# Attention heads in units of three instead of two: transposes of P, products with V, V rows at a pitch of 40, and a new order

## The chip, the cores and the metric

The kernel runs on one core of one Trainium2 chip. The metric is the device time of one execution in microseconds, the median of the runs shown; lower is better. TensorE (PE) does the matrix products and transposes, VectorE (DVE) and ScalarE (ACT) work between PSUM and SBUF, GpSimd (POOL) and SyncE (SP) issue DMAs.

## The reference

Four layers follow one another on x of 2048 rows by 512: attention A, gated FFN B, A again, B again, each with a layer norm before it and its input added. A walks over 64 segments of 32 rows. Each segment is joined to 8 memory rows, and the memory rows of the next segment are the first 8 output rows of this one, so the segments must be done in turn.

```
for s in range(n_seg):                      # 64, one after another
    h = concatenate([mem, xs])              # 8 + 32 = 40 rows
    q, k, v = h @ Wq, h @ Wk, h @ Wv        # 32 heads of 128
    p = softmax(where(mask, q k^T * scale, -1e9))
    o = (p v) @ Wo
    mem = o[:, :8]; outs.append(o[:, 8:])
B: (sigmoid(x w_gate) * (x w_up)) @ w_down  # 512 -> 1792 -> 512
```

## The kernel before

**Steps.** `emit_step` (L858) does one step: segment t of the first attention layer and segment t - 6 of the second side by side, as 2 x 40 = 80 columns. There are 70 steps; steps 6 to 63 hold both layers, the first and last six one layer. All weights of A lie in SBUF; the FFN weights are streamed by POOL in pieces (L1152, L1153, L1177). `ffn` (L1113) runs for four segments at a time (a block), and its matmuls, the V passes of coming blocks (`v_pass`, L716) and the layer norms are what TensorE can do while a step waits for itself.

**Heads.** The 32 heads are taken as 16 units of two: head u and head u + 16. Three units make a group of six heads, so a step has five groups of six and one of two (L497 to L499). For a group: Q and K (L935), copied to `qku` by ACT; scores (L970); on DVE mask, maximum, subtraction (L984, L989, L991), exponential on ACT (L994), sum, reciprocal, product (L996, L998, L1001), which leaves P in `pb` with each head in 64 columns; one transpose a unit (`ptr`, L1013), which turns the two heads of a unit to partitions 0 to 39 and 64 to 103; two copies (`spread`, L1017) to `ptsb`, which put each head in columns of its own and zero in the rest (`lower` is 0 above the second head's rows, 1 below); the products with V (`pvm`, L1040), one a unit and layer; a copy to `otsb`; and the output projection (L1058). The sum of all heads gives the next step's memory rows (L1071).

**V rows.** `vsb` holds the V rows that a step multiplies: three tiles of half the heads, two used a step. The second head of a unit lies 64 partitions below the first. Rows of x are computed ahead by `v_pass` and lie in DRAM (`scr`); eight DMAs a step with both layers fetch them (L904). The memory rows and the rows around them are computed in the step (`strips`, L849: 32 matmuls into four strips of 32 partitions, eight heads each), copied to the one tile `sst`, and sent to `vsb` by eight DMAs (L915) in the order of halves.

**Order.** Every task (some instructions on one engine) has dependencies, and the list SEQUENCE, a packed permutation, gives each a priority. `forward` (L287) plays the tasks through with planned durations, always taking the first in priority that can go, and so sets each engine's program order. Where the plan leaves TensorE waiting over 250 ns and its use around that gap is under 60%, `warm` (L432) puts matmuls on the tile `hot` in (at most 512 columns each, shown at L1283), which compute nothing that is used.

Of the kernel before, what the change touches and what calls it, by code (L numbers as in the profile page):

```python
# [54 lines left out]
;AsOkoLv9`|Nk$f)V(EM&}eu|$fC*urB1ZmLCVnbIiO{+HzA9)1<7?iu49pb(F}QJGi)Mg^0?ej9TT%>AnXGip&#Uz1Yr8{%{!1PcqJ{qbHL*46O=`m^O8{4Ag{5mcV_X)uOki698u=JbnecdQ)K?*jal`5k@vgq  # L55
O#U-a+Y~cLsg}0BaD;=R(uf~+cDuOTj@JKC;Rp|!BSTrXhnGGEu2%?g?J3{5u2N_9c4_%y>Rv3GR3tbZ)35VLYb%41oUy#Ihn<M~Q_0PVJfBAjNN{?ArwdoxQl<8vGoCwW00SsIKwToFeLh}80qVHqyuc{BDH}Ey
{H^GH#mhlWktNfVUA_ObdEE8yLY~EY#;q0uJyla@^F8xlDxTf&iV#}}k%IRd<x89?fY<{VoG&ZiZDAtha3$KRH{_E2=pj7Ub)bKc&g{kv{=p<B33H2I%(GM876q}G|L&{(rXf+CSLenR2oySHQ8ncu>TnKY{XhT1
?TMKCCm-VE^y=fng`^uZ+^sDt13Z<=jDIP{P3xVKz`!ct$wx2qkoT>eyRST`@>$Zc6F@P+mW6XGY9+$Vs<`x|H(D!?ZBEBql0MU9kT4Rr?<%pVq&RX$KUAD(slP|owV&{0j(-#4d*u#-q|9w-%@MpethdTH$qkCd
6|IG;_iy1dNi<{8R<Y-t*Z7AcN`{y1Zc5;TSUhrMfVfA-_-6}JgtI8A#Q1E=b`WOK5^~&mS{dK4ku8CFRO{TIv63+=(P?6CsuH-+?-Q$b*;V;v7g8oR+f?V};zlQm*%~HtiTbPS>i#JSHN&MilwlzAf#lGrX4(5o
JrCuU{~<^*{mnSblJbT~tZg;n6sKkmCneGTjg20ED^mjHd?@}zwiJ}QxH0g5BDw7pD3%0?;2T;EAWpDb?2J~GfZlUEDCCSg0q)`5yKb(GbdD3}^G^OmVj^dF*y@ih1|qzn>2at0(c7q;$}c9252(bzy0&q@E~Sv*  # L60
GXhk);r*_V=wc=7DFhq1t0^|jR*Hm_QlTqOW;fO`YPVL>=v^%wub=xW?P*i1%~Ob!M&(+_FK_e#vFRTC@r8>s#^u<%CZA8iji*hKiCGt?DjdVOn5tH+`KgLfYpiiCwt1w4j-LstcC$+~w;F-=IuU3;1Oq$VvaOVU
_S{vk%=q!AFI?;DuNc4b2yMJ+2*o9xG9ib$oOpD}s7@VYnma-~c{H>^>!GDpwojb;Bk~AstXZ*m`<`^1oc^Ao#v3ALTiO^PvrXJ~Kp#rUkMj6$`bMLe+xGUlSxQ5sO@$l$(B8<vz!~B1)5ZoV<1$<wj*GX?HIYjL
(A3~WrpA$or6&VL_xici_S7a9+v9%=y0hu!p|er(?}aXw{LdjCua%iOF7B4yTzSrHxwdgZF@u4l9m--GD-3T43nLR~TP^CAb_Mvm2n(K6%eA)Hi3mzK_H6`=r|y-#@HXj<!hgX>L~_bBe_^v~n3&Fa;|!BdB$aF^
?UwyG$lcfh@iLd>l@=8<Iye-jrf`vgT+E}lE|IV0(UY)o2daV&{Cheo!bTrqkMEpwnaG8qtrDP&p-sDO#XTJB{6-p(`Z|%6$9d(56?0>}Hnvb;I}1Hcww2uD*w-iv-~3Pv7>ptX+AT|E4mR1+5eZ5$?wttv&uHLR
1dgfX{P5n((GDeT;c$jo&C4ioc`nV}E)U44AaI#?c4xlgWj~q!d3EUFbp@HFP)P!KwmR8Gt7o|+q6N>%0!h{`s!F`1TRo4rdNGu}b4XbS7Y4kZDtGd`F=kM=-X`xYk3{;qj@mdET|`MuNhb^0(FlWjLoFZwlbspr
f*z`Tk!FkgDa0HM5$G%}cr!#+S>=;wt0mLGroaKT_r$I#s7Mhnpa!lC^q$lbH48m3a<sCo#-=q0n*^Sys%L_3+F8-1tPHF_Gx5C&Gf%pg{eXNi)6N01;g=+vhb*;Nnd1b<OfPd`;D#nyxvqiVG|O8#1DS7$<tB^E
NIL3erxaCpiBh4~i`21Sjv+m=yO=O<8GGg)rmuk?+PE)r`4Pz%AHd10rIzDlfC6n)S-|9VpoPePn-Tz7%@bxy(Vo<zW*m&1B<WP{nSREA2Jfs*&7zo&qz{z(4;<s0U|q7yxHgKws=ZLIGY@^C6S%dpL+o!xSP}>~
1^anNE}jYpLB_6(S_Ao8OZgz<WCPa*mZf;~An4=j0~fx(hIAyg`-kss;*I0f>kE)-bmx`Dr%0OpTPKDhv<HGdB^nJWIthe8MJ=!0+3iERRaWt|_pBw*R3T`&%|47GbLRPr8;AGi`9fU0hi9L3RPV>=+YUXM-#e@C
@1A#@s;uT+%_?u?1y}+|vp>>i1^gK<r;enb80tVX9Q!HtL6t;PGOO!&rgWh4wWLr~n(#~=N=4?k&om$D*}zCzdjUPbsE*)!Yli^o=6##Vh(!E*Fv@-R#Lz>+A^AlRl9zz!*<Hc}?ayVBH&JAwms75uI<?T+UkaqQ
UF02QasyU|1;o6=UyH-imTIrGtM=|{sv<}Od)cxP%0K^tLm5;XY@OGucPB%W485G2=`jxAA*A?5jR`^9R`)`ZC0g4Gm$hD=n)&o#<IS7(#|CYXnNOWjBjWdVT01~zIN-epto-Mr=t|R1HemE8#@M<@8?HBtPmw6M  # L70
H~p3D0=P8Kr7lS(@A!8*+J9Vcj_@RpmyYg0Ao=nE&*`{$_xquaS^S7CxtA`#+onhks4U%V_C>Ni>p0VJg1G#<sK70daQ~+!3d0KXjhR@lGe*X(PltJH75(%U+_~RxhVpGQi^4$V{k2taQ{(mXR}(AgnVMKb=m>Z)
ewpv8M}ar=+ak{0UJ!_yRQfmtbx?t3`H~&;{ur58BJp_Cdp1JGBDw5s4e#66qO-^CsbMCep+WUN5}jky#v6OibJ*!g+k#Q~2gnL^Pat**eTqqT#>K{0gCQk%B}dBT2Cg?Q$-L8t8ur4{Xx*jwy%zuqu#j*U&ORwB
q%tQEi-vR?4g6hdG5a1gv>Kuvrht>h@v<tF4ncn+p4&hdUu~=%n=1&Dak36wjj%?XP>O@U&($c)ZRxy9p4h9_t(^Mkw>`<Dg<}|P{KU#!GD3=&^zditEjxaJQ-)d4(uHu@#g&Uz@%xy79+QPaqqTSWQ*>Z8qVL{I
1_#0b2AS)7SZLJpO(uEk)(b+8=BT_q6hR9>RKC4t<m4ME*C=B-Ah?cwDCV8_u?@kLm9L^0P3Gb>X~8^!<n~~H<)qX}UKBd;C4E6t!9d_IcQK1<XqLzV56-mb>Ut5KqX}?hbiw+1aQUP}3+n+|fR!>AHTckh5CHK7
A|^7r4BupK)p1t{D(XlquV)sysuLpa*v68G-#(<b#-S}o*zN-S;OnyrU-7obFX!O|W4%;Uj+GT+T@f9osMr-bv$DwR<e;R@+(rg=u;%sSP-~4CI}ugoIRIQJ16$4{bWtp7ZxU`$zTcqO^0bdrXA@x_NbbnYAVoic
$6#csoA@80l?l`+G0UJb2eQkn+HJc-z{__<nNGs!rMGHd*b;KH=d6~BEkOB@hk6fo3dk8h_H-!@IHEIC1h&o6vx$Ie<qyw<t~&^^pTdz9jW-1r4cqKB<PAq0jPF|VD@w7Wn+$&TX%9~+b0qmb2fO1e6>a<8Q5`R2
>ABezR@U}(@aoA2pz{3u)>l&0ySVhwMRaTg@6J^o?W`>zWTDc~MvENf`u+40C%DKP%Y~L%LyLc|<ikb^YBcUc7j{|@aFg6A=QhL=<F8q{jbWi;bfc~v@SFXQvAo~EnPp9_&VNNdWvs9=PRWhgJ%OkfbiIWe7a7=i
FDmuxoNdd#e4+I99cv2m?Pv2$b2xV+ec^;+HDx}nJun_B?HTr$Rp9Z$Ck~EIJGI;H!~g-koU=YNZ#J^teR1Ix-kqhNMSeJ|!uw?vBqp4RK(I{O{WmSauU+?HaFXM>_=`9&!x2fRJZlxAFN7o=3-WIExWihbgiWIh
7I>W<07<NMXHvJ&Y26oHmqhJNA0`xtbB-1z!S$}U)$O1@B=@ERfx}yW^b}QJ`J8B>{0S2x&05vHXUeg)OJ4{Z?}87ke=_GSohFoUiu%%yoit#ESi@9~_Zd|a(az_UG<MWAgf_q_L0_`<<sM6=jZ(7025qc&cq$D&
dc%HbKfgTkfwDQkbO2m|#)Rn_NYmxV+*q6rqa^_HuF}1hrNP7^N%fFR%7%+p7{i;A#1-pz1Auv)Ufx28PEP8A8w^tnHjYeJBp~3d5Z3`?xxz9kcBua|G}m()#^TbGZNU>@3tClz=-8!ohmh(YSmZUa+c2HlGf2{M  # L80
%=$ceF_)Zv*HLi~=R#=+rN~V3Ejuew4<YmxBOkK->7o$9-rQFVPIn?OZ@YW3ZV=dI9l{Kx$zd^}NA~+QSf6~kdnx(q0gbi&Vz<n}b?1Y}1Y9G{7Pr-JSNv_M$Stl0JvOON;uPce=n;i6-aqMMZ>FNZgZ1SshdoD5
T&a3gEi9*n>qkTsxXsR{`Cr6jz04c$|6IK{r_}#FmMI9Dv0z5ezQdu;`dR+8k4(FxPrI|t3vD}hK-uG}`lrHeh`&4h#R$ikG%sLCw;TG4k5H-Igi*#|$)Pl|Zw+UfyY+MUKw=Hwp!<~oJVk%MzbfAp9YtFqoNWXZ
Vk-{`mfT&9=`-c-7~^<W!jMPR8uXHrsy<C6A~5hpsKj`|Uao&M1>Lw%YnQaeiQs8ti@t2n6<C27iOXVKmL5!;MH;7&wZ}??vXK(qSjE}wIVyRBXbvBZ-IR^T3lK;wBkxq(1`_q<vX3pYpi}0_>0^4S2sxU<X=(n?
)AIBS#-6>k*cd_SHLM~A)v%?kE|XUGLSIk9vPMsu;w?kHH@%}{7Y%>8HfHEgw1fmn3)DCxCT23S$KJ`yST(8CI3Hz@fZ|@KLgW8=fHa32O_&W2IwFZj#`K!W#;8>Ce_$qc8@kVjiFO3I#xit?gotIf2k?R0%%-Ob
lhln?Xi2EdGbl(~!0}0^<CvBVwC*~zt+Uf`=d&>nglS7(n39NVEJe>UPrcl3ktD8OKph~rssP^Xiew@d0z&3ir08G|N=W&03@OViOgG_t=0pKPnZ?9<rG8s|<>Wp&YZCtY;2x9SA1I;hDm^H*!XQj&cBm1c5<|Iv
)Pm74sdZ-+;|L$~max>Sa_w@h=MjVRrAmw?S%dzo>sPWdVfiguEOmvWs&M<xHZ?yf(D!BZydSVEL%}aIaocLLM{o8*U@ub?5td;*!!|M9hY-I}2dXzf!Q7U8iBSa64a|!1&X0nn<3E{uTJ~U=R9njs@urQ@8fS{f
zirfGnyQ4a8suz1z_;)M%kQG5nFV+g{YHeLj5Lq=>;7Y0RS)L|_=NA955WW48wHiH>S{V3Zm}+%4@h@K2g!aahDSWo<BM6w^{YX12ICdYrij-`LW$+|b&|&eCG3Eim{!LRoL%~`$L&Oh`@loZ$`o$pqrg+)T5|(>
$-$PuYQOYl1hM2jZFpiL5T9cJ=)R%`Gd9w-<Apss-226onD;>_t{mc!NbZH(krC+lNKSDeEfDwi9{+fsy(PdkTy;nZ3EF}gbXV9y0h5GW^6gIAswDgt)c10#g`L$exUKvJbfTjQW)}YVQoD>>H(AqhZkO*6v9CI|
_(E@w*FmagFtyfnx$r<RFu_Mg1Byt2598@E+uU9d?$Kon*Jj5lyikh|uFRKl&`w3@r|U%F0|3yo!G~ynrNoEO*MF?OEPQK-=-B|CpyBIe-1cqxK;26#)fH_gTo<j?Q4qPlNoGvqOKv3YU(4=PHxfsIWr4`ZmZM5R
kc+hD>7{*O@<mO;9d&|ZuMT6hIy^B#U}bJ%!btuf`$QrAJ>;<I7Gr~3NRs6{51bo<I)>B+|8+~Mgm}5mF(#yzQM9`pPlVO)=r@Gelq8qoMM-Fir|L@tZ3|e1$9kNp_-|VN+V@Dn0!|(gryFf1P8~SeE6MY$K~M)|  # L90
# [385 lines left out]
class Kern:  # L476
# [126 lines left out]
    def load_weights(self):  # L603
# [10 lines left out]
        for h0, n in ((0, 4), (4, 4), (8, 4), (12, 4), (16, 4), (20, 4), (24, 4), (28, 4)):  # L614
            cs = slice(h0 * P, (h0 + n) * P)
            tk = ld(self.wv[:, :, cs], wv_v[:, :, cs], P * self.DC * n * P * 2, [("wv", h) for h in range(h0, h0 + n)], [("wv", h0 - 8)] if h0 > 4 else [])
            if h0 > 4:
                tk.after = pl.writer[("wv", h0 - 8)]
# [744 lines left out]
```

## Time and profile before

| what | value |
|---|---|
| three timed runs | 1776.6, 1775.84, 1775.11 us |
| median | 1775.84 us |
| span of the profiled execution | 1771.0 us, granted clock 1.000 |
| median less span | 4.8 us |
| PE, PEld, DVE, ACT, POOL busy | 99, 85, 66, 66, 33% |
| L1013, transposes of P | 1120 |
| L1040, products with V | 2048 |
| DMA | 273.43 MB, mean 154 GB/s |

The span runs from the first to the last instruction of the execution that was profiled; what of its own time lies outside the span is not shown, and the timed runs stand 4.8 us above it. PE is TensorE's matmuls, PEld its weight loads, which overlap them. The duration of one matmul includes its way through the pipeline and overlaps the next; in the chain that ended last, matmuls stand with the time from one issue to the next.

### The profile page before, as it was taken

The numbers are of one execution on the slowest core, as the hardware profiler recorded it, in microseconds if no ns is written. First come the engines' busy times: TensorE is split into PE (matmuls) and PEld (weight loads), VectorE is DVE, ScalarE is ACT, GpSimd is POOL, SyncE is SP. The second block draws the span as 40 slices with busy tenths as digits, with TensorE's granted clock in tenths as the row PEclk, the third lists the DMA queues.
The fourth block names the chain that finished last, engine by engine and source line by source line (L and its number), as shares of the span: only waits on it lengthen the run. The fifth ranks groups of instructions, "written<-read, shape, count | busy, mean of one in ns | idle before, by whom it ended". The sixth has DMA issues, their size and how long they took to land.

```text
span 1771.0 us, 92273 instructions
## 1 busy us (share of the span) xinstructions
PE 1755.7 (99%) x40066; PEld 1509.6 (85%) x40066; DVE 1174.8 (66%) x4018; ACT 1166.2 (66%) x3024; POOL 577.8 (33%) x836
## 2 busy tenths in 40 slices
PE   9999999999999999999999999999999999999998
PEld 4678888889888888989898898989889888989886
DVE  4477676777566666766776667667766765676665
ACT  6676766666666666666666667666666666666664
POOL 5413032522333242313334241333324232333432
PEclk9999999999999999999999999999999999999999
DMA  9835254634555464445546453555546444554543
GB/s 354 275 88 169 73 165 138 206 109 130 155 158 162 126 193 134 142 123 164 165 143 184 130 172 107 155 155 169 155 131 192 125 139 127 162 153 136 170 135 108
DMA packets 135113, 273.43 MB, mean 154 GB/s; under 512 B 30778, under 2 KB 68546, under 8 KB 134706
## 3 DMA queue, kind: packets, MB, share of 16 engines
q0 software_dynamic: 56656, 183.09, 34.5%
q1 hardware_dynamic: 78050, 84.43, 16.4%
q8 instruction: 314, 5.14, 1.2%
q14 instruction: 93, 0.76, 0.2%
HBM read 221.78 MB, written 27.07 MB: 141 GB/s over the span
## 4 chain that ended last, share of the span: by engine, by line
PE 96%; DVE 1%; ACT 1%; SPq 0%; issue 0%; DMA 0%; POOL 0%; ACTq 0%; DVEq 0%; POOLq 0%
PE bank L935 33%; PE bank L1058 17%; PE bank L1160 11%; PE bank L724 8%; PE bank L849 7%; PE bank L1183 6%; PE bank L970 4%; PE bank L1040 4%; PE bank L1013 2%; PE bank L684 1%; PE bank L1283 1%; PE bank L1128 1%; SPq L915 0%; DMA vsb<-sst 0%; PE bank L762 0%
## 5 line engine op out<-in xcount | busy, mean ns | idle before, releaser
L935 PE MATMUL bank<-hT,wq_sb 128*128 128x80 bf16 (+3 forms) x8960 | 615.2, 198 | 0.8 <-issue 0.4
L935 PE MATMUL bank<-hT,wk_sb 128*128 128x80 bf16 (+3 forms) x8960 | 614.8, 198 | 0.0
L1297 ACT CAST qku<-bank 128x480 bf16<-128x480 f32 (+3 forms) x770 | 387.3, 506 | 219.3 <-PE bank L935 180.2
L935 PEld LDWEIGHTS <-wq_sb 128*128 128x128 bf16 x8960 | 452.3, 99 | 21.4 <-issue 10.6
L935 PEld LDWEIGHTS <-wk_sb 128*128 128x128 bf16 x8960 | 446.7, 99 | 0.0
L984 DVE TENSOR_TENSOR st<-bank,cst 40x240 f32<-40x240 f32 (+3 forms) x768 | 279.1, 368 | 166.6 <-PE bank L970 160.0
L1058 PE MATMUL bank<-otsb,wo_sb 128*128 128x80 bf16 (+1 forms) x8960 | 361.0, 198 | 1.9 <-ACT otsb L1297 1.1
L1058 PEld LDWEIGHTS <-wo_sb 128*128 128x128 bf16 x8960 | 336.0, 99 | 17.3 <-issue 2.8
L1153 POOL DMA_DIRECT2D wu<-in_B_w_up_dram x217 | 164.0, 756 | 275.8 <-PE bank L1160 91.6
L1152 POOL DMA_DIRECT2D wg<-in_B_w_gate_dram x217 | 164.0, 756 | 234.4 <-PE bank L1160 164.4
L1297 ACT CAST otsb<-bank 128x480 bf16<-128x480 f32 (+3 forms) x420 | 198.0, 483 | 62.1 <-PE bank L1040 43.4
L1177 POOL DMA_DIRECT2D wd<-in_B_w_down_dram x217 | 153.7, 709 | 217.5 <-PE bank L1183 72.0
L994 ACT ACTIVATE st<-st 80x240 f32<-80x240 f32 (+3 forms) x420 | 158.7, 381 | 37.5 <-DVE st L991 34.8
L996 DVE TENSOR_REDUCE small<-st 80x6 f32<-80x240 f32 (+3 forms) x420 | 150.6, 362 | 37.3 <-ACT st L994 35.7
L674 POOL TENSOR_TENSOR small<-small,cst 128x1 f32<-128x1 f32 (+1 forms) x80 | 44.9, 562 | 397.9 <-DVE small L673 392.1
L1160 PE MATMUL bank<-xnT,wg 128*128 128x128 bf16 (+2 forms) x1784 | 171.8, 218 | 0.1
L1160 PE MATMUL bank<-xnT,wu 128*128 128x128 bf16 (+2 forms) x1784 | 171.0, 218 | 0.0
L970 PE MATMUL bank<-qku 128*128 128x80 bf16 (+1 forms) x2240 | 162.2, 198 | 0.4 <-ACT qku L1297 0.4
L991 DVE TENSOR_TENSOR st<-st,small 80x240 f32<-80x240 f32 (+3 forms) x420 | 154.5, 370 | 4.2
L1001 DVE TENSOR_TENSOR pb<-st,small 80x240 bf16<-80x240 f32 (+3 forms) x420 | 153.3, 369 | 4.2
L989 DVE TENSOR_REDUCE small<-st 80x6 f32<-80x240 f32 (+3 forms) x420 | 151.6, 363 | 4.5
L1040 PE MATMUL bank<-ptsb,vsb 104*128 104x80 bf16 x2048 | 136.0, 199 | 2.9 <-DMA vsb<-sst 1.2
(107 smaller groups left out, 2399.6 us busy)
## 6 DMA issues: line engine op xcount, KB each, us to landing
wg<-in_B_w_gate_dram POOLq DMA_DIRECT2D x220, 256.0 KB, 4.3
wu<-in_B_w_up_dram POOLq DMA_DIRECT2D x220, 256.0 KB, 4.1
wd<-in_B_w_down_dram POOLq DMA_DIRECT2D x220, 256.0 KB, 4.1
vsb<-scr SPq DMA_DIRECT2D x460, 48.0 KB
vsb<-sst SPq DMA_DIRECT2D x464, 32.0 KB
scr<-vst SPq DMA_DIRECT2D x112, 96.0 KB
wv_sb<-in_A_Wv_dram SPq DMA_DIRECT2D x8, 512.0 KB
wo_sb<-in_A_Wo_dram SPq DMA_DIRECT2D x10, 384.0 KB
```

Of the source, the lines that this page charges most:

```text
L935: nc.tensor.matmul(o_ap, lhsT=W[:, c, h * P:(h + 1) * P], rhs=mv(c), start=(c == 0), stop=(c == DC - 1))
L970: nc.tensor.matmul(s_all(SB)[:, w0 + i, :], lhsT=fview(qku[:, i, 0, 0:1], [(1, P)]), rhs=qku[:, i, 1, 0:ncol], start=True, stop=True)
L984: pl.add("DVE", dve_ns(n, True), lambda gsz=gsz, hs=hs, st=st, SB=SB, pj_=pj_, npj_=npj_, mk=mk, idx=idx: nc.vector.tensor_tensor(out=st[p ...
L991: pl.add("DVE", dve_ns(n), lambda gsz=gsz, hs=hs, st=st, mx=mx: nc.vector.tensor_tensor(out=st[pr, hs], in0=st[pr, hs], in1=mx[pr, hs].uns ...
L994: pl.add("ACT", act_ns(n), lambda hs=hs, st=st: nc.scalar.activation(out=st[pr, hs], in_=st[pr, hs], func=ACTF.Exp, scale=self.scale), r=s ...
L1040: nc.tensor.matmul(fview(OB[:, o:o + 1], [(ncol, 2), (1, L)]), lhsT=self.vsb[halves[u // 8]][0:64 + L, j, (u % 8) * P:(u % 8 + 1) * P], rh ...
L1058: nc.tensor.matmul(WB[:, c * ncol:(c + 1) * ncol], lhsT=self.wo[:, h, c * P:(c + 1) * P], rhs=otsb[:, hl, 0:ncol], start=(h == 0 and c == ...
L1152: pl.add("POOL", 760, lambda wg=wg, fs=fs: nc.gpsimd.dma_start(out=wg[:], in_=self.wgv[:, :, fs]), r=[("wo", self.H - 1)], w=[gk] + bt, la ...
L1153: pl.add("POOL", 760, lambda wu=wu, fs=fs: nc.gpsimd.dma_start(out=wu[:], in_=self.wuv[:, :, fs]), r=[("wo", self.H - 1)], w=[uk] + bt, la ...
L1160: nc.tensor.matmul(gu[:, 2 * i + k, 0:n], lhsT=W[:, c, i * P:(i + 1) * P], rhs=xnT[:, c, rw], start=(c == 0), stop=(c == DC - 1))
L1177: pl.add("POOL", 760, lambda wd=wd, ip=ip: nc.gpsimd.dma_start(out=wd[:], in_=self.wdv[:, 2 * ip:2 * ip + 2, :]), w=[dk] + (["boot"] if se ...
L1297: nc.scalar.copy(out=dst, in_=src)
```

## The change

Three rows of heads (0 to 10, 11 to 21, 22 to 31) take the place of two; a unit is one head of each row, so there are ten units of three and one of two. Groups are two units, again five groups of six heads and one of two. A unit's P lies in 3 x 40 of 128 columns; one transpose turns three heads to partitions 0, 40 and 80 on; three copies spread them; one product a unit and layer has up to 120 rows and 120 columns. `vsb` becomes two tiles, each with all heads of a step, three rows of heads at a pitch of 40 partitions; no rows between them need zeros any more. The strips keep eight heads of each row in three strips and the other eight in the fourth, so each row gets two DMAs from `sst`: one of 1024 columns and one of 384 or 256. `runs` gives the pieces in which the columns of `wv`, now in the order of the strips, stand for heads in order; the writes to `scr` and the loads of `wv` are cut by it. SEQUENCE is new. The copies from `kx` wait for the step's `hT` as well.

```diff
-        for u in range(0, self.HH, 3):
-            us = list(range(u, min(u + 3, self.HH)))
-            self.groups.append(([h for k in us for h in (k, self.HH + k)], us))
+        self.NU = (H + 2) // 3
+        self.row_heads = [list(range(i * self.NU, min((i + 1) * self.NU, H))) for i in range(3)]
+        for u in range(0, self.NU, 2):
+            us = list(range(u, min(u + 2, self.NU)))
+            self.groups.append(([r[k] for k in us for r in self.row_heads if k < len(r)], us))
+        self.full = 8 * P
...
-        self.NV = 3
-        self.vsb = [c.tile([P, 2, 1024], BF16, name=f"vsb{i}") for i in range(self.NV)]
-        self.pb = [c.tile([LW, HG, 64], BF16, name=f"pb{i}") for i in range(3)]
-        self.ptsb = [c.tile([P, HG, 2, L], BF16, name=f"ptsb{i}") for i in range(3)]
+        self.NV = 2
+        self.vsb = [c.tile([P, 2, self.NU * P], BF16, name=f"vsb{i}") for i in range(self.NV)]
+        self.pb = [c.tile([LW, 2, P], BF16, name=f"pb{i}") for i in range(3)]
+        self.ptsb = [c.tile([P, 2, 2, 3, L], BF16, name=f"ptsb{i}") for i in range(3)]
...
+    def runs(self, k, w):
+        out = []
+        for i, r in enumerate(self.row_heads):
+            n = len(r) - 8
+            for p0, m, s0 in ((0, 4, 8 * i), (4, 4, 8 * i + 4), (8, n, 24 + 3 * i)):
+                lo, hi = max(s0, 4 * k), min(s0 + m, 4 * (k + w))
+                if lo < hi:
+                    h = r[p0 + lo - s0]
...
-            for hf, vh in enumerate(halves):
-                for i in range(0 if j and not s else 2):
-                    h0 = i * self.HH + 8 * hf
-                    pl.add("SP", 430, ...  # vsb[vh][row:row + nx, j, :] <- scr[j], heads h0 to h0 + 7
+            for i, rh in enumerate(self.row_heads):
+                m = len(rh) * P
+                pl.add("SP", 430, ...  # vsb[vh][row:row + nx, j, 0:m] <- scr[j], heads of row i
...
-            for i4 in (0, 2, 1, 3):
-                vh, i = halves[i4 % 2], i4 // 2
+            for k in (0, 1):
                 for j, lo, k0, nr, name in parts:
+                    for i in range(3):
+                        p0, o, m, c = (32 * i, 0, self.full, 0) if not k else (96, 3 * P * i, (len(self.row_heads[i]) - 8) * P, self.full)
+                        pl.add("SP", 632, ...  # vsb[vh][L * i + k0:..., j, c:c + m] <- sb[p0 + lo:..., o:o + m]
...
-                           r=kk, w=[(qku, "e")], use=[qku])
+                           r=kk + hkeys, w=[(qku, "e")], use=[qku])
...
-                    nc.tensor.transpose(out=pt[:, ul * LW:(ul + 1) * LW], in_=pb[full, 2 * ul:2 * ul + 2, :].rearrange("p i k -> p (i k)"),
+                    nc.tensor.transpose(out=pt[:, ul * LW:(ul + 1) * LW], in_=pb[full, ul, :],
...
-            for i in (0, 1):
+            for i in range(ni):
                 def spread(i=i, nu=nu, ptsb=ptsb, PB=PB):
-                    r = slice(0, 64 * i + L)
+                    r = slice(0, L * (i + 1))
...
-                        nc.tensor.matmul(fview(OB[:, o:o + 1], [(ncol, 2), (1, L)]),
-                                         lhsT=self.vsb[halves[u // 8]][0:64 + L, j, (u % 8) * P:(u % 8 + 1) * P],
-                                         rhs=ptsb[0:64 + L, ul * nj + idx, :, :], start=True, stop=True)
-            vk = [(n_, j, vh, i) for vh in sorted({halves[u // 8] for u in us}) for j in jobs for n_ in ("vs", "vx") for i in (0, 1)]
+                        nc.tensor.matmul(fview(OB[:, o:o + 1], [(ncol, ni), (1, L)]),
+                                         lhsT=self.vsb[vh][0:L * ni, j, u * P:(u + 1) * P],
+                                         rhs=ptsb[0:L * ni, ul, idx, 0:ni, :], start=True, stop=True)
+            vk = [(n_, j, vh, i, k) for k in sorted({int(u >= 8) for u in us}) for j in jobs for n_ in ("vs", "vx") for i in range(ni)]
```

More of the change, by code (lines that the diff above doesn't have):

```diff
@@ L595, in clear @@
         for k, t_ in enumerate(self.ptsb):
-            pl.add("POOL", 440, lambda t_=t_: nc.gpsimd.memset(t_[:], 0.0), w=[("ptsb", k, i) for i in (0, 1)])
+            pl.add("POOL", 440, lambda t_=t_: nc.gpsimd.memset(t_[:], 0.0), w=[("ptsb", k, i) for i in range(3)])
         for k, t_ in enumerate(self.qku):
             pl.add("POOL", 440, lambda t_=t_: nc.gpsimd.memset(t_[:], 0.0), w=[("qkz", k)])
-        for k, t_ in enumerate(self.vsb):
-            pl.add("ACT", 1760, lambda t_=t_: (t_[32:64], fview(self.hot[32:64, 0:1], [(0, 2), (0, 1024)])),
-                   w=[(n, j, k, i) for n in ("vs", "vx") for j in (0, 1) for i in (0, 1)])
     def load_weights(self):
@@ L613, in load_weights @@
         xb = list(self.boot_x)[1:]
[L614 to L618, printed above, removed]
+        for k in range(self.H // 4):
+            h0 = 4 * k
+            for o, c0, m, _ in self.runs(k, 1):
+                h1 = h0 + o // P
+                tk = ld(self.wv[:, :, h1 * P:h1 * P + m], wv_v[:, :, c0:c0 + m], P * self.DC * m * 2, [("wv", h) for h in range(h1, h1 + m // P)], [("wv", h0 - 8)] if h0 > 4 else [])
+                if h0 > 4:
+                    tk.after = pl.writer[("wv", h0 - 8)]
             if h0 == 0:
@@ L623, in load_weights @@
             xb = xb[2:]
[L624 to L626 removed]
+        for u0, n in ((0, 2), (2, 4), (6, 5)):
+            hs = [r[u0:u0 + n] for r in self.row_heads]
             for nm, sb, v in (("wq", self.wq, wq_v), ("wk", self.wk, wk_v)):
[L628 to L634 removed]
+                for r in hs:
+                    cs = slice(r[0] * P, (r[-1] + 1) * P)
+                    ld(sb[:, :, cs], v[:, :, cs], P * self.DC * len(r) * P * 2, [(nm, h) for h in r])
+            for r in hs:
+                ld(self.wo[:, r[0]:r[-1] + 1, :], wo_v[:, r[0]:r[-1] + 1, :], P * len(r) * self.D * 2, [("wo", h) for h in r])
+    def runs(self, k, w):
[6 more added lines that the diff above has]
+                    h = r[p0 + lo - s0]
+                    keys = [(i, p0 + q - s0) for q in range(lo, hi)]
+                    if out and out[-1][1] + out[-1][2] == h * P and out[-1][0] + out[-1][2] == (lo - 4 * k) * P:
+                        o, c0, m0, k0 = out.pop()
+                        out.append((o, c0, m0 + (hi - lo) * P, k0 + keys))
+                    else:
+                        out.append(((lo - 4 * k) * P, h * P, (hi - lo) * P, keys))
+        return out
     def first_qk(self):
@@ L891, in s_all @@
             return B[:, 0:6 * ncol].rearrange("p (h k) -> p h k", h=6)
-        halves = [self.nxt("vsb", self.NV) for _ in range(2)]
+        vh = self.nxt("vsb", self.NV)
         alone = not both and t - j0 * LAG in self.thin[j0]
@@ L900, in emit_step @@
             lo, nx = (2 * 8 * j, 8) if alone else (0, XS)
-            for hf, vh in enumerate(halves):
-                for i in range(0 if j and not s else 2):
-                    h0 = i * self.HH + 8 * hf
-                    pl.add("SP", 430, lambda j=j, s=s, row=64 * i + row + lo, h0=h0, vh=vh, r0=s * XS + lo, nx=nx: nc.sync.dma_start(
-                        out=self.vsb[vh][row:row + nx, j, :], in_=self.scr[j][r0:r0 + nx, h0 * P:(h0 + 8) * P]),
-                        r=[("vd", j, b, q, kk) for q in range(lo // 8, (lo + nx) // 8) for kk in (h0 // 4, h0 // 4 + 1)] + ([("wo", self.H - 1)] if t == 0 else []), w=[("vx", j, vh, i)], lat=2700.0, nb=nx * 2048, slow=0.9)
+            for i, rh in enumerate(self.row_heads):
+                if j and not s:
+                    continue
+                m = len(rh) * P
+                pl.add("SP", 430, lambda j=j, row=L * i + row + lo, h0=rh[0], m=m, r0=s * XS + lo, nx=nx: nc.sync.dma_start(
+                    out=self.vsb[vh][row:row + nx, j, 0:m], in_=self.scr[j][r0:r0 + nx, h0 * P:h0 * P + m]),
+                    r=[("vd", j, b, q, (i, k)) for q in range(lo // 8, (lo + nx) // 8) for k in range(len(rh))] + ([("wo", self.H - 1)] if t == 0 else []),
+                    w=[("vx", j, vh, i, k) for k in (0, 1)], lat=2700.0, nb=nx * m * 2, slow=0.9)
         def add_strips(col, parts):
             sb = self.strips(lambda c: hT[:, c, col:col + 32], skeys)
-            for i4 in (0, 2, 1, 3):
-                vh, i = halves[i4 % 2], i4 // 2
+            for k in (0, 1):
                 for j, lo, k0, nr, name in parts:
@@ L1058, in wom @@
                             nc.tensor.matmul(WB[:, c * ncol:(c + 1) * ncol], lhsT=self.wo[:, h, c * P:(c + 1) * P],
[L1059 removed]
+                                             rhs=otsb[:, hl, 0:ncol], start=(h == 0 and c == 0), stop=(h == self.groups[-1][0][-1] and c == DC - 1),
                                              skip_group_check=True)
@@ L1107, in last_weights @@
                     pl.add("POOL", 760, lambda tl=tl, src=src: nc.gpsimd.dma_start(out=tl[:, :, :], in_=src), w=keys, lat=4700.0, nb=370000,
-                           r=[("vs", 1, (2 * (self.NSTEPS - 1) + q) % self.NV, i) for q in range(2) for i in range(2)] if k else [])
+                           r=[("vs", 1, (self.NSTEPS - 1) % self.NV, i, q) for q in range(2) for i in range(3)] if k else [])
                     row.append((tl, own))
```

357 lines of the change are left out of this document (199 added, 158 removed).

## The prediction

> **What bounds the kernel now.** I read the page's busy table first, then the chain that ended last, then the chain inside one ordinary step, then the stages without spare work.
>
> ```profile
> span 1771.0 us, 92273 instructions
> PE 1755.7 (99%) x40066; PEld 1509.6 (85%) x40066; DVE 1174.8 (66%) x4018; ACT 1166.2 (66%) x3024; POOL 577.8 (33%) x836
> PE 96%; DVE 1%; ACT 1%; SPq 0%; issue 0%; DMA 0%; POOL 0%; ACTq 0%; DVEq 0%; POOLq 0%
> ```
>
> TensorE is busy all the time and the chain is TensorE work to 96%; VectorE and ScalarE have a third of the span free. So a matmul less is time less, wherever TensorE is never short of work. The price of a matmul is its step in the chain, not its duration (199 ns for the transposes of P at L1013 and for the products at L1040), because matmuls overlap. The chain between 900 and 926 us, an ordinary step:
>
> ```profile
> 902.52 0.11 PE bank L1013 x3
> ...
> 903.39 0.90 PE bank L1160 x16
> 904.29 0.43 PE bank L1040 x12
> ```
>
> Three transposes take 0.11 us (36.7 ns each), twelve products of 80 columns 0.43 us (35.8 ns each), sixteen FFN matmuls of 128 columns 0.90 us (56.3 ns each). On the line through the last two, 120 columns cost 52.9 ns.
>
> Where there is little other work, the stages differ:
>
> ```profile
> 118.60:135.40 16.80, 16.35 (x498) 13.80 (x494) 10.86 (x41) 12.01 (x46) 2.12 (x3) 1.00 0.29 84
> 175.60:200.10 24.50, 24.50 (x548) 19.41 (x541) 14.98 (x56) 18.35 (x47) 0.17 (x1) 1.00 0.33 91
> 200.10:221.30 21.20, 19.66 (x509) 16.90 (x506) 13.73 (x53) 15.25 (x42) 0.00 (x0) 1.00 0.25 66
> ```
>
> Each line is one step (columns: length, then PE, PEld, DVE, ACT, POOL). Step 6 (second line) has no idle TensorE at all; step 7 (third line), with no FFN beside it, has 1.54 us. In step 3 (first line) part of "busy" is filler: the matmuls on `hot` (L1283) that the code puts where its plan leaves TensorE waiting. The chain of step 7 says what it waits for:
>
> ```profile
> 207.47 1.79 SPq L915
> 209.26 0.05 issue
> 209.31 0.58 SPq L915
> 209.90 0.04 issue
> 209.94 0.59 SPq L915
> 210.53 0.04 issue
> 210.57 3.26 DMA vsb<-sst
> 213.83 0.14 issue
> 213.97 0.56 PE bank L1040 x11
> ```
>
> The V rows of the memory and of the rows around it are computed in the step itself (L849), copied, sent to `vsb` one DMA after another by SP (about 0.6 us each), and land 3.26 us after the last needed issue; only then the first product runs.
>
> **The change part by part.** The order of instructions of the changed kernel gives the counts, the rows above the prices.
>
> Transposes of P: 16 a step become 11, in all 1120 become 770. They still stream 80 columns. 350 x 36.7 ns = -12.8 us.
>
> Products with V: 2048 of 80 columns (73.3 us at 35.8) become 1280 of 120 and 128 of 80 (67.7 + 4.6 = 72.3 us): -1.0 us. The columns are the same; only a fixed part of 768 - 128 = 640 matmuls goes. With V rows at a pitch of 40, 120 rows are contracted instead of 104; the row with 128 rows (56.3 ns) is on the same line, so nothing for that.
>
> A rule is weighed here. The rows give 36 ns at 80 columns, weight load included (85% of PEld is busy beside it). The Trainium skill (TensorE: Matmul & The Clock Gate, "Back-to-back issue gap") says that in a stream of weight loads and matmuls the spacing is set by both, about 81 ns at 128 columns and 131 ns at 512. By a line through these, 74.7 ns at 80 and 79.9 at 120, the two terms would be -26 and -41 us, and the time some 1709 us. The trace disagrees with it at 128 columns, 56.3 against 81 ns, so the sum goes by the rows.
>
> Filler matmuls: 92 become 133, 42,624 columns become 61,184. A filler of 1664 columns takes 0.71 us in the chain at 101.83 us, 0.427 ns a column: 18,560 columns are +7.9 us. They sit in step 6 (+2.5 us), in step 61 (+1.4), in 63, 65, 68 and 69 (+2.8 together), and 0.3 to 0.5 each in the boot, steps 1 to 5 and step 7. These are the places where less TensorE work leaves a wait for something else. Step 6 had no idle time, so its filler is new. Step 7 and steps 65 to 69 had waits already, which filler can only replace. Bounds: 0 (all of it replaces waits) and +10.7 (all new, and each of 14 more filler blocks leaves the 0.2 us that 27 such blocks leave on average now). I take +6.9: step 6 is the nearest row to a fresh wait and its filler counts in full, as do the others but for 1 us that replaces waits the late steps had.
>
> Spread of P (L1017): two copies a group of six heads become three, each of 160 elements instead of 240. From the rows for 80 and 240 elements (ACT 215 and 347 ns plain, 325 and 460 scaled; DVE 187 and 270, 246 and 331) the new ones cost 281, 392, 228 and 289 ns, and with the counts by engine ACT gets +74 us, DVE +12 us over the run, about 1.2 us a step. It is hidden: ACT goes from 66 to 70% of the span, and the last group of a step, which the end of the step hangs on, has two heads and still two copies. Without that cover it would be some 0.25 us a group. 0 on the path; end of the range +4 (0.25 us in sixteen filler-less steps).
>
> V rows: `vsb<-scr` 508 DMAs become 381 (356 ns of SP each), `vsb<-sst` 516 become 774 (587 ns each): SP gets -45 + 151 = +106 us, 1.5 us a step, on a queue that waits over 340 us for L1040 to give `vsb` free. The first product of a step with both layers now waits for six strip DMAs instead of four: 2 x 0.63 = 1.26 us later. What hides it is the TensorE work put between strips and first product. In the order of before, by the rows, that is 6.3 us in step 7, 7.1 in the next, 9.3 in the median; in the changed order 6.7, 7.9 and 11.2. The waits of the last three heads of a unit row (the second piece of 384 or 256 columns) fall on groups 4 and 5, 10.6 us or more after the strips. Two whole-step tiles instead of three halves: a tile is free when the step before the last has done its products, no earlier need than before. I take +0.5 (step 7), end +18 (below).
>
> Boot: up to the first QK of step 1 both orders hold the same V passes, strips and heads; the changed one puts more V passes ahead of step 0, and 1,280 filler columns more (counted above). The three ScalarE clears of `vsb` (1.89 us each) go; they ran beside filler. DMA is full for the first 60 us (share 1.02 to 1.09), and the weights come in other pieces: 0, ends -2 and +3. One more dependence (the kx copies of steps 6 to 11 wait for the step's hT) sits beside the 0.86 us of QK matmuls that the same copy waits for: 0.
>
> Sum: -12.8 - 1.0 + 6.9 + 0.5 = -6.4 us. The profiled execution's span is 1771.0 us; the three timed runs have the median 1775.84, 4.8 us more, which lies outside the span and which I leave alone. 1775.8 - 6.4 = 1769.4 us.
>
> **The rivals.** (a) All of the saving: the added filler only stands where TensorE waited before. For it: steps 7, 61, 65, 68 and 69 had waits. Against it: step 6. -13.8 + 0.5: 1762.5 us.
>
> (b) Nothing gained: with 0.2 us less of TensorE a step, softmax on DVE and ACT becomes what every filler-less stretch waits for, ACT with 1.2 us a step more. For it: step 3, where TensorE needs filler already. Against it: in 903 to 1006 us TensorE is busy 103.00 of 103.00 while ACT is busy 67.13. The sum would be -13.8 + 10.7 + 4 = +0.9: 1776.7 us.
>
> (c) Slower: the V rows come late. Place: the wait of L1040 for `vsb<-sst`. Six issues need 1.4 (strip end to first issue done, as in step 7) + 5 x 0.63 + 2 to 3.3 us of landing = 6.5 to 7.8 us after the strips. It decides when landing under the larger number of DMAs takes 5 us, a need of 9.5: then the ten both-layer steps with 6.7 to 9.0 us between lose 1.26 us each on average, and the eight single-layer steps (5.2 to 6.2 us between, three DMAs first instead of two) 0.63 us each: +18. 1769.4 + 18 = 1787 us. For it: the chain of step 7, and smaller pieces. Against it: the row of L1040 has 1.2 us of idle released by `vsb<-sst` in the whole run, in two places. The Trainium skill (DMA: Bandwidth & Descriptors, "Anatomy of one DMA") says a DMA has about 2 us of fixed cost whatever its size, so that splitting does not make pieces land earlier; the 3.26 us agrees in kind.
>
> That the change does not do what it says is settled by the order: the counts are as told.
>
> **How the numbers follow.** About 0.2% (3.6 us) is what a measurement of this kernel can tell from no change. Forecast 0.48, (a) 0.20, (b) 0.17, (c) 0.15. The forecast's own range, 1764 to 1774, is faster but for its last microsecond or two. Faster 0.66, same 0.17, slower 0.17. The range takes in (a) with the boot's -2 and (b) with its +3, and leaves (c) out: 1760 to 1779.7.
>
> **What would show it.** Right: the transposes at 770 with 37 ns in the chain, products of 120 columns at 53 ns, steady steps 0.2 us shorter with TensorE still full, step 6 longer than that saving by filler. Wrong: idle before L1040 released by `vsb<-sst` in many steps (c); idle TensorE at ACT or DVE in 903 to 1006 us (b); a boot that ends more than 2 us away from 84.3 us.

## The result, and the profile after

The changed kernel is slower: 1797.7 us as the median of its runs beside 1776.2 of the kernel before, a ratio of 1.0128 (95% interval 1.0107 to 1.0149). The forecast was 1769.4 us with a range that ended at 1779.7; rival (c), late V rows, had given 1787. The profiled execution of the changed kernel took 1800.13 us with a span of 1798.3.

The page of the changed kernel, the lines that answer to those shown of before:

```profile
span 1798.3 us, 91097 instructions
PE 1762.6 (98%) x39117; PEld 1504.5 (84%) x39117; DVE 1170.9 (65%) x4093; ACT 1204.4 (67%) x3294; POOL 589.1 (33%) x861
PE 88%; DMA 4%; SPq 3%; DVE 2%; ACT 2%; issue 1%; POOL 0%; DVEq 0%; ACTq 0%; POOLq 0%
```

TensorE has 949 matmuls less and is counted busy 7 us longer. The chain has gone from 96% TensorE to 88%, and what came in is SyncE's queue and DMA, which stood at 0%. The waits of TensorE, longest in total first (us in total, times, longest), say at which line:

```profile
PE bank L1112 <- DMA vsb<-sst: 6.9, 10, 1.2
PE bank L1112 <- issue: 5.3, 4, 2.1
PE bank L1200 <- ACT oxT L1369: 4.3, 11, 0.5
...
PE bank L1112 <- DMA vsb<-scr: 2.6, 2, 1.7
```

L1112 is the products with V. The kernel before had this line for them (L1040):

```profile
PE bank L1040 <- DMA vsb<-sst: 1.2, 2, 0.6
```

So the matmuls were saved, and TensorE now waits for V rows in front of the products; how much of the loss that is, the experiments show. The chain between 921 and 924 us has the prices of the new matmuls:

```profile
923.20 0.07 PE bank L1085 x2
923.27 0.21 PE bank L1112 x4
```

35 ns a transpose, 52.5 ns a product of 120 columns: the forecast had 36.7 and 52.9. If each matmul of the two traces is given its step by columns (columns / 2.4 plus 2.4 ns; strips by their measured step), the sum goes from 1721.6 to 1715.4 us, filler included: -6.2 us. What TensorE took beyond that sum, from its first matmul to its last, went from 44.7 to 78.2 us: +33.5. A gap is here the time from one matmul's issue to the next, less the step of the first; the gaps of over 60 ns in front of products went from 7.3 to 22.7 us in that part.

One step shows the mechanism. The chain in step 14 of the changed kernel (start, us, what):

```profile
393.47 0.07 PE bank L1085 x2
393.54 0.45 PE bank L1232 x8
393.99 0.06 PE bank L1112
394.05 2.08 issue
396.13 0.32 PE bank L1112 x3
```

Between two products TensorE stands for 2.08 us. The page calls it "issue", but the strip transfers of that step tell what it was. On SyncE (durations min, median, max in ns, then first and last start):

```profile
L985 SPq DMA_DIRECT2D vsb<-sst x12: 573/588/1980, 385.9 to 394.8; - x12
```

By the length of their rows they went out as wide, wide, narrow, wide, wide, wide, wide, narrow and four more narrow. Wide is 2048 bytes a row, six of which the first product needs; narrow is 768 or 512 bytes, which only groups 4 and 5 need. The third issue, a narrow one, took 1.98 us. The sixth wide one was issued by 391.7 us, 0.4 us after a 256 KB load of `wu` and just ahead of one of `wg`, and its last part landed 4.35 us after its issue, at 396.0. Then the second product ran.

Step 14 is no exception among the 58 steps with both layers: the six wide transfers stand first in seven of them only, the last of the six is issued 8.3 us after the strips and lands 10.4 us after them (medians; the latest 14.4). In the kernel before, with the order of its instructions laid beside its trace, the last of the four that the first product needs is issued 5.2 us after the strips and lands 7.7 us after them (medians). The prediction had 6.5 to 7.8 us for the landing of the six.

### The profile page after: what moved, and what is told of

Its sections match the earlier page's. It is cut to its first block, busy times and chain, and to the rows that moved or that the text cites. A ratio compares the mean times of both kernels' runs of the same rounds, so it can differ in the third digit from the quotient of the medians.

```text
span 1798.3 us, 91097 instructions
## 1 busy us (share of the span) xinstructions
PE 1762.6 (98%) x39117; PEld 1504.5 (84%) x39117; DVE 1170.9 (65%) x4093; ACT 1204.4 (67%) x3294; POOL 589.1 (33%) x861
## 3 DMA queue, kind: packets, MB, share of 16 engines
q0 software_dynamic: 56992, 182.89, 34.8%
## 4 chain that ended last, share of the span: by engine, by line
PE 88%; DMA 4%; SPq 3%; DVE 2%; ACT 2%; issue 1%; POOL 0%; DVEq 0%; ACTq 0%; POOLq 0%
PE bank L1005 30%; PE bank L1130 17%; PE bank L1232 10%; PE bank L791 8%; PE bank L916 7%; PE bank L1255 5%; PE bank L1112 4%; PE bank L1040 4%; SPq L985 2%; DMA vsb<-sst 2%; PE bank L1085 1%; PE bank L751 1%; PE bank L1355 1%; DMA vsb<-scr 1%; PE bank L1200 1%
## 5 line engine op out<-in xcount | busy, mean ns | idle before, releaser
L1369 ACT CAST qku<-bank 128x480 bf16<-128x480 f32 (+4 forms) x770 | 388.6, 507 | 204.9 <-PE bank L1005 171.4
L1224 POOL DMA_DIRECT2D wg<-in_B_w_gate_dram x217 | 164.0, 756 | 274.5 <-PE bank L1232 169.4
L1225 POOL DMA_DIRECT2D wu<-in_B_w_up_dram x217 | 164.1, 756 | 244.1 <-PE bank L1232 80.0
L1249 POOL DMA_DIRECT2D wd<-in_B_w_down_dram x217 | 154.1, 711 | 181.2 <-PE bank L1255 58.7
L1361 ACT ACTIVATE ptsb<-bank,small 80x160 bf16<-80x160 bf16 (+3 forms) x540 | 186.7, 375 | 22.9 <-PE bank L1085 15.1
L741 POOL TENSOR_TENSOR small<-small,cst 128x1 f32<-128x1 f32 (+1 forms) x80 | 44.7, 559 | 446.3 <-DVE small L740 443.7
L1040 PE MATMUL bank<-qku 128*128 128x80 bf16 (+1 forms) x2240 | 162.8, 198 | 2.8 <-ACT qku L1369 2.7
```

Of the source, the lines that this page charges most:

```text
L1040: nc.tensor.matmul(s_all(SB)[:, w0 + i, :], lhsT=fview(qku[:, i, 0, 0:1], [(1, P)]), rhs=qku[:, i, 1, 0:ncol], start=True, stop=True)
L1224: pl.add("POOL", 760, lambda wg=wg, fs=fs: nc.gpsimd.dma_start(out=wg[:], in_=self.wgv[:, :, fs]), r=[("wo", self.H - 1)], w=[gk] + bt, la ...
L1225: pl.add("POOL", 760, lambda wu=wu, fs=fs: nc.gpsimd.dma_start(out=wu[:], in_=self.wuv[:, :, fs]), r=[("wo", self.H - 1)], w=[uk] + bt, la ...
L1249: pl.add("POOL", 760, lambda wd=wd, ip=ip: nc.gpsimd.dma_start(out=wd[:], in_=self.wdv[:, 2 * ip:2 * ip + 2, :]), w=[dk] + (["boot"] if se ...
L1361: nc.scalar.activation(out=dst, in_=src, func=ACTF.Copy, scale=by)
L1369: nc.scalar.copy(out=dst, in_=src)
```

## The experiments

Ratios are to the kernel before on the same chip; where two experiments are compared, it is by their ratios times 1775.8 us. "Gaps" are those of over 60 ns in front of products, as above, summed from a trace.

**The order of the strip transfers.** TensorE's order is kept, and each slot of SyncE's queue too.

```
+ def wide_first(self, order):
...
+         slots = sorted(at[i] for _, i in ks)
+         new = sorted(ks, key=lambda e: (e[0], at[e[1]]))
...
```

> The changed kernel, with TensorE's order and every slot of SyncE's queue kept, but in the slots that a step's twelve strip transfers hold, the six wide ones (2048 bytes a row, needed by the first product) go first and the six narrow ones (768 or 512 bytes, needed by the last two groups) after. In the trace of the changed kernel the sixth wide transfer is issued some 8 us after the strips and the sixth slot stands at some 5, so this brings the last row that the first product needs forward by about 3 us. Theory 1, the order on SyncE: of the 22.3 us in front of products most goes, and with the waits of 2 us the 7 us at half clock: 1797.7 - 12 to - 20, 1778 to 1786 us. Theory 2, twelve transfers are too many in whatever order: a gain of at most 5 us, 1793 to 1797. Theory 3, the loss lies outside the V rows (shapes, copies that put the thirds apart, filler matmuls): 1797 within 2.

Measured: 1789.1 us, 1.0074 (1.0052 to 1.0096), 9.6 us less than the changed kernel. The sixth wide transfer is now issued 5.2 and landed 7.5 us after the strips (medians), what the prediction had counted on, and the gaps fall from 22.7 to 15.5 us. Less went than theory 1 alone would have it. Of the 11.1 us that TensorE still sits idle in front of products by the waits that the profile lists, 9.7 are in four places:

```profile
PE bank L1113 <- DMA vsb<-scr: 5.0, 2, 3.6
PE bank L1113 <- DMA vsb<-sst: 4.7, 2, 3.7
```

Both long ones have the same form. In step 34 the chain comes out of SyncE's queue and waits for a transfer to land:

```profile
906.49 0.36 SPq L972
906.85 0.04 issue
906.90 3.63 DMA vsb<-sst
910.52 0.01 issue
910.53 0.39 PE bank L1113 x3
```

In step 18 it runs along the queue too, through strip transfers and a write of `scr`, and then waits 4.01 us for rows from `scr`. So order is a part of it, the length of the queue and the landing are others.

**No strip transfers at all.** In both kernels L985 (L915 before) issues nothing from step 10 on.

> The changed kernel without its strip transfers from step 10 on (the strips are still multiplied and copied, but their rows of V stay those of older steps: this part of the computation is left out). Products then wait only for rows from the scratch buffer. Theories 1 and 2: the wait in front of products and the half clock after it go, and the kernel stands where the sum of its matmuls puts it, 6 us under the kernel before without strip transfers: 1765 to 1775 us. Theory 3: 1790 or more, at least 15 us above the kernel before without strip transfers.

> The kernel before without its strip transfers from step 10 on (the same part of the computation is left out), as the partner of the changed kernel without them. The kernel before waited 1.2 us for strip rows on TensorE, so all theories expect little: 1770 to 1776 us.

Measured: 1776.0 us, 0.9995 (0.9986 to 1.0004), and 1772.0 us, 0.9978 (0.9969 to 0.9988). The strip transfers cost the changed kernel 23.6 us (1.0128 less 0.9995) and the kernel before 3.9. The gaps fall from 22.7 to 6.1 us, and up to 6.8 us of loss at half clock (last section) go with them, together about as much. That is 20 of the 28 to 29 us by which the forecast was too low. The waits of the changed kernel without them:

```profile
PE bank L1112 <- DMA vsb<-sst: 1.1, 3, 0.5
```

But it stands 3 to 4 us above its partner, not 6 below: a second part of the miss, some 10 us, has nothing to do with strip rows. Theory 3, that the loss lies outside the V rows, is true of that part.

**Twelve transfers in the kernel before.**

```
- [... vsb[vh][64 * i + k0:..., j, :] <- sb[32 * i4 + lo:..., :, :]]
+ [... for c, m in (((0, 512), (512, 512)) if i4 < 2 else ((0, 1024),))]   # columns c to c + m
```

> The kernel before, with the strip transfers of the first sixteen heads cut in two of 512 columns each, so that a step issues twelve strip transfers and not eight, and its first product needs six and not four. All else as before. Theory 1, the order: the narrow pieces here all stand before or among those that the first product needs only where they are needed, but the sixth comes some 1.2 us later than the fourth did, and the kernel before waited 1.2 us in all for such rows: 1776 + 0 to 6 us. Theory 2, the number of transfers itself: most of the loss of 22 us shows here too, 1788 to 1800. Theory 3: 1776 within 2, since neither number nor order matters.

Measured: 1845.1 us, 1.0378 (1.0358 to 1.0397). No theory had it so bad. The gaps are 64.7 us, 34 of them in front of the first two products of a step, and the chain:

```profile
PE 77%; SPq 10%; DMA 7%; DVE 2%; ACT 2%; issue 2%; POOL 0%; DVEq 0%; ACTq 0%; POOLq 0%
...
PE bank L1041 <- DMA vsb<-sst: 38.5, 37, 3.8
```

An order that was made for eight transfers has no room for twelve: a product waits in 37 places. The changed kernel, whose order was made with twelve in the plan, loses 23.6 us at its strips, about a third of these 67. It also shows that the kernel before was nearer to its edge than its 1.2 us of waiting told.

**Fewer things on SyncE.** Two repairs on top of the wide-first order: the narrow transfers moved back behind what is more urgent, and the narrow transfers on GpSimd.

```
+ cap[d] = min(cap.get(d, 1e9), tk.start - (7000.0 if tk.on == "PE" else 1500.0))   # a_late, d a narrow one
...
+ key[tk.idx] = (max(last, cap[tk.idx]), n)
...
+ order.sort(key=lambda tk: key[tk.idx])
- nc.sync.dma_start(...)                           # a_pool
+ (nc.gpsimd if c else nc.sync).dma_start(...)     # c is above 0 for the narrow ones
```

> As the kernel with the wide strip transfers first, and each narrow one moved back in SyncE's queue to 7 us before the product that needs it is due by the plan (behind writes of scr and loads from scr that stood after it). In the wide-first kernel two products wait 3.7 and 3.9 us, in steps 18 and 34, where narrow transfers and writes of scr stand ahead of loads that are needed sooner. Theory 1, what stands ahead on SyncE: those two waits and most of what follows them go, 1776 to 1783 us. Theory 2, landing behind the feed-forward weights whatever the queue's order: 1786 to 1792. Theory 3, the number of transfers on SyncE in whatever order: 1786 to 1792 too, and the trace tells the two apart by whether the late row was issued late or landed late.

> As the wide-first kernel, with the six narrow transfers of a step issued by GpSimd and not by SyncE, at the same places of the order. SyncE is left with six strip transfers of 0.59 us a step. Theory 1 and the theory of the number on SyncE: 1775 to 1783 us. Theory of the weights: the narrow ones now stand among the weight loads of GpSimd's queue and hold them back, with late weights in front of the feed-forward matmuls: 1788 or more.

Measured: 1794.2 us, 1.0111 (1.0094 to 1.0128), against all three theories, and 1784.2 us, 1.0044 (1.0031 to 1.0056), just above what theory 1 gave. In a_late the waits have moved: 7.4 us of the gaps stand in front of the first product that needs a narrow row, which the wide-first kernel waited 0.8 us for. Seven microseconds from planned issue to need are too few. In a_pool SyncE's issues take 36% of the time between 90 and 1670 us, where they took 52% in the changed kernel and 43% in the kernel before, and the long wait for strip rows is gone; GpSimd pays with 197 us more of busy time than in the changed kernel:

```profile
PE 1743.9 (98%) x38928; PEld 1498.6 (84%) x39117; DVE 1169.2 (66%) x4093; ACT 1200.4 (67%) x3294; POOL 786.1 (44%) x1248
...
PE bank L751 <- DVE xn L742: 4.6, 5, 1.9
PE bank L1201 <- ACT oxT L1385: 4.3, 11, 0.5
PE bank L1113 <- DMA vsb<-scr: 3.3, 2, 2.9
```

(Some matmul records are missing from this trace.)

**The feed-forward weights.** L1224, L1225 and L1249 load one row of 512 or 1024 bytes where they loaded 256 KB.

> The changed kernel with the feed-forward weights' loads cut to a row of 512 or 1024 bytes each after the first that fill the buffers, so that the feed-forward layers compute with old weights (that part of the computation is left out); the number of loads and their order stay. Theory 2, the collision with 256 KB loads is a necessary part: strip transfers land in 1.2 to 2.7 us in place of up to 4.4, and 8 to 15 us of the loss go: 1783 to 1790 us. Theory 1 alone, late issue on SyncE: at most 4 us go, 1793 to 1797. Theory 3: 1796 to 1799.

> The kernel before with the feed-forward weights' loads cut in the same way (that part of the computation is left out), as the partner of the changed kernel with thin loads. It waited 1.2 us for strip rows and 0.4 us for gates, so all theories expect 1770 to 1776 us.

Measured: 1785.4 us, 1.0047 (1.0029 to 1.0066), and 1772.4 us, 0.9980 (0.9971 to 0.9988): 14.4 us less for the changed kernel, 3.6 for the kernel before. The wide strip transfers land in 1.39 us (median; 2.12 in the changed kernel), nine in ten within 2.9 (3.6), although they are issued just as late (8.4 us after the strips). The collision with the loads is a part of the loss, but not one that is new: in the kernel before the same transfers land in 1.8 us (median; 3.2 in nine of ten), and in 1.4 with thin loads. What is new is that the last needed one goes out 3 us later, so that a slow landing is no longer covered. The Trainium skill (DMA: Bandwidth & Descriptors, "Anatomy of one DMA") puts about 2 us of cost on a DMA whatever its size, for DMAs that GpSimd issues; these are SyncE's. In size the runs agree (narrow pieces land in 2.4 us where wide ones take 2.1), but the cost is no constant: 1.4 us with thin loads, up to 5.2 beside full ones.

**All repairs together.**

> The changed kernel with the wide transfers first, the narrow ones on GpSimd, and the thin feed-forward loads (the feed-forward layers compute with old weights, that part is left out). If late issue on SyncE and late landing behind the weights are together the whole loss at the strips, it stands where the kernel without strip transfers stands, or lower by the 3 us that thin loads gave the kernel before: 1772 to 1777 us. If there is a third part, 1780 or more.

Measured: 1774.6 us, 0.9993 (0.9984 to 1.0002). With the wide ones first, the narrow ones off SyncE and the loads thin, the changed kernel stands where it stands without strip transfers (thin loads gave the kernel before 3.6 us, so up to that much may still be lost). Late issue and late landing are nearly the whole loss at the strips. Taken one after another, the order gave 9.6 us, the narrow ones off SyncE 5.3 more and the thin loads 9.1 more; each depends on those before it, since thin loads by themselves gave 14.4.

**The reordering on the kernel before,** with its second four transfers left on SyncE or given to GpSimd.

> The kernel before, with the four strip transfers of a step that the first product needs put in the first four of their eight slots: the reordering of the wide-first kernel, done on the kernel before. The kernel before without strip transfers stood 3.3 us lower, so there is little to win: all theories 1772 to 1777. A gain like the 8.6 us of the changed kernel would say that the reordering is a repair for both and not for what the change did.

> The kernel before, with the four strip transfers that the first product needs first, and the other four issued by GpSimd: the repair of the changed kernel done on the kernel before. The kernel before without strip transfers stood 3.3 us lower and with the needed ones first 1.7 us lower. If SyncE's load still costs it something: 1772 to 1774 us, faster than both kernels. If GpSimd's weight loads suffer: 1776 to 1780.

Measured: 1774.3 us, 0.9991 (0.9982 to 1.0000), and 1774.5 us, 0.9994 (0.9985 to 1.0002). The needed transfers are out of order in the kernel before as well (by the order of its instructions they stand first in one of its 57 steps 7 to 63), but putting them first gains at most 3 us there and cannot be told from nothing: with eight transfers the slack covers it. No version here that does the whole computation beats the kernel before by an amount that can be told.

**The part that is not strips.** Three kernels without strip transfers from step 10 on: each transpose twice, no filler after the boot, no third spread copy from step 10 on.

```
+ for ul in [k for k in range(nu) for _ in (0, 1)]:                                     # a_dbltp
+ fill = {k: v for k, v in self.pl.warm(order).items() if self.pl.tasks[k].start < 95000.0}   # a_nofill
+ ... spread if i < 2 or t < 10 else (lambda: None)                                     # a_nothird
```

> The changed kernel without strip transfers from step 10 on (1776.0 us), with each of its 770 transposes of P issued twice into the same place. The prediction put 36.7 ns on a transpose, all of it on the path. If that holds, 770 x 36.7 = 28 us more: 1804 us (1800 to 1808). If TensorE has slack around the softmax chain, as the rival of no gain had it, 1776 to 1790.

> The changed kernel without strip transfers from step 10 on (1776.0 us), without the 84 filler matmuls after the boot (15.6 us of issue time by their rows). If they stand in holes that the work leaves anyway, nothing is gained, and without them the clock falls in the holes: 1774 to 1782 us. If they push real work back, as the prediction's sum had it when it added their time, up to 1761.

> The changed kernel without strip transfers from step 10 on (1776.0 us), and from step 10 on also without the copy that spreads the third head of each unit (its P stays that of older steps: this part of the computation is left out), so that a group has two spread copies as in the kernel before. The prediction priced the third copy at nothing, hidden beside TensorE, with 4 us as the bound. Hidden: 1774 to 1777 us. If the third copy carries the rest of the loss, 10 us between the sum of the matmuls and the time: 1766 to 1771.

Measured: 1799.5 us, 1.0135 (1.0121 to 1.0149): +24.9 us by the ratios, +23.5 by the medians, 31 to 32 ns for each of 770 transposes, so that TensorE has next to no slack around them. (The groups of the two traces show how little the duration of one, the 199 or 200 ns after the busy time, says of that price.) The rows, without and with the doubling:

```profile
L1085 PE MATMUL bank<-cst,pb 80*128 80x80 bf16 x770 | 95.6, 200 | 0.1
```

```profile
L1085 PE MATMUL bank<-cst,pb 80*128 80x80 bf16 x1540 | 122.8, 199 | 1.3
```

The filler: 1777.4 us, 1.0009 (0.9999 to 1.0018): without 15.6 us of filler nothing is gained, it stands in holes. One stretch of 3.4 us at half clock, in step 3, came in its place; that is 1.7 us at most, and hides no gain of the filler's size. The third copy: 1772.3 us, 0.9983 (0.9974 to 0.9992), 2.1 us less by the ratios, 3.7 by the medians, and as the two intervals touch, it costs between nothing and 4 us; it fell between what the two theories gave.

## Why the prediction was wrong

The mechanism that it feared, rival (c), is what came; what failed is the step by which it was given 0.15.

- **V rows, +0.5 with the end at +18: measured about +20** (23.6 less 3.9). The failed step is "Six issues need 1.4 (...) + 5 x 0.63 + 2 to 3.3 us of landing = 6.5 to 7.8 us after the strips". It took the six that the first product needs to be the first six that SyncE issues. They are in 7 steps of 58; the last of them lands at 10.4 us in the median, against 11.2 us of TensorE work set between strips and first product. With wide first it is 7.5, inside the prediction's figure. The order is 9.6 of the 20 us; the rest went with the narrow transfers on SyncE and the landing beside the weight loads, which the step had at 3.3 us at most and which took up to 5.2. The order of instructions shows the scramble; the prediction took from it counts and TensorE's work, but not where the six stand.
- **"Decides when landing takes 5 us":** too strict for the same reason. Landing had a median of 2.1 us and 3.6 in nine of ten; late issue did the rest. The price of (c), +18, was close by luck: it was put on eighteen steps of 0.6 to 1.3 us each; six single steps (14, 18, 26, 28, 30, 50) hold half of the gaps.
- **"Against it: the row of L1040 has 1.2 us":** an idle time of 1.2 us says that rows come in time, not by how much. The kernel before with twelve transfers waited 38.5 us at that row.
- **Transposes, -12.8, and products, -1.0: right in kind.** Between the two kernels without strips the transposes went from 45.3 to 34.8 us of issue time, -10.5, 2 us short of the term; doubling them gave 31 to 32 ns each in place of 36.7. Products: -1.5 us by columns.
- **Filler, +6.9: about right as the size of holes.** Its issue time went from 23.4 to 33.6 us, +10 with 2 us of it in the boot. It stands in holes, since taking it out gained nothing. Rival (a), that these are only waits of before and the whole saving stays, falls: without strip transfers the changed kernel stands above its partner.
- **Spread copies, 0 with the end at +4:** measured 0 to 4, left open within that. Their extra time on the engines was counted rightly: ScalarE's copies to `ptsb` went from 195 to 269 us, VectorE's from 85 to 99.
- **Boot (what comes before step 1), 0 with the end at +3: +3.1.** The first QK matmul of step 1 starts at 88.4 us of the span, where it had started at 85.3. The prediction had named a boot that ends more than 2 us off as a sign of being wrong.
- **What no term had:** matmuls at half clock behind stalls of 2 us (below), some 7 us, a part of the 23.6.
- **The rule of the Trainium skill** on the spacing of weight loads and matmuls (TensorE: Matmul & The Clock Gate, "Back-to-back issue gap"), which gave 1709 us: the new products agree with the trace of before and not with the rule, 52.5 ns at 120 columns where the line through the page's two figures has 80.

Outside the strips the changed kernel lost some 10 us against the sum. Boot 3, transposes 2, the third copy 0 to 4 and small waits for the tile `oxT` (5.1 to 6.7 us in front of L1200, L1128 before) and in front of the scores make up about that; they are read from traces, and no run took the boot or `oxT` alone. The outcome of this part is rival (b)'s, nothing gained, and a part of its mechanism too (the copies and `oxT` are ScalarE's), but not the idle time in 903 to 1006 us that it named: there TensorE without strip transfers is busy 103.00 of 103.00 us.

## What to carry to other kernels

Cutting transfers differently changes a queue, and a queue has an order: before a time is put on "the n-th transfer", list which transfers the waiting instruction needs and where they stand in the queue of the changed program. A wait that is near zero in the profile gives no measure of its slack; adding a few transfers to the kernel before would have shown how thin it was. If a change saves work on the bounding engine and adds to the queue that feeds it, price the feed first.

## What the hardware showed beyond that

A stall of 2.1 us could be enough to lower TensorE's clock. After the stalls in steps 14 and 30 (2.1 to 2.2 us, in front of a product) matmuls ran at twice their step and the granted clock is 0.50 for 3.41 us; in step 18 (2.1 us in front of a feed-forward matmul and 1.9 in front of a product, with half a microsecond of work between) it is 0.50 for 6.83 us. The window around step 18 in the changed kernel, and the same stretch without strip transfers (length, PE, PEld, DVE, ACT, POOL, granted clock, DMA share, GB/s):

```profile
506.00:513.00 7.00, 5.50 (x73) 5.53 (x74) 1.88 (x9) 2.99 (x8) 1.95 (x3) 0.54 0.42 125
```

```profile
506.00:513.00 7.00, 7.00 (x170) 6.21 (x170) 2.25 (x6) 3.39 (x9) 2.92 (x4) 1.00 0.92 256
```

Half clock for 13.7 us in all costs up to 6.8 us; the kernel before and the changed one without strip transfers have no such stretch between boot and end. So a late transfer of 2 us can cost nearer to 4 us.

Not every stall does it. With the narrow transfers on GpSimd TensorE waits 2.9 us for rows from `scr` at 504 us, and the granted clock stays 1.00. The stretches of the other traces show why that can be. In each trace they begin on a grid of 3.413 us: in the changed kernel the second is 32 steps of it after the first (109.23 us) and the third 91 after the second (310.61 us), and the ten of the kernel before with twelve transfers lie on one grid too. If the gaps of the five traces with such stretches are summed by grid cell (after the boot, cells at full clock), every cell with 2.1 us of gaps or more is followed by half clock and none with less than 1.5 us; between these both occur. So it counts how much of a stall falls into one cell. The trace of a_pool has no stretch to lay the grid by, so for its own wait this is not shown. The Trainium skill (TensorE: Matmul & The Clock Gate, "The HAM clock gate") has the clock halved after an idle window of about 3.4 us; the length agrees with the grid, but here a window that was idle for some 2 us of it was enough.

The size of a transfer within SBUF hardly mattered: pieces of 8, 12 and 32 KB had the same 0.59 us of issue on SyncE, and landed in 2.45, 2.35 and 2.12 us (medians). Six narrow ones cost the queue as much as six wide ones.
